# Linear attention ahead of two expert layers on one Trainium2 core: chunks 8 to 23 laid out by head group, with 8 loads a chunk instead of 15

## The chip, the core and the metric

The kernel runs on one core of a Trainium2 chip. The metric is device time in microseconds. One execution was taken by the hardware profiler; its trace is the source of every row below. The engines are TensorE (PE: matrix multiplies; PEld is its weight load), VectorE (DVE), ScalarE (ACT), GpSimd (POOL) and SyncE (SP), which here only issues DMAs.

## What is computed

Three stages follow one another over 3072 tokens. The first is attention with a decaying state, 4 batches of 8 heads of 768 steps, 64 wide; its output is the input of the second.

```python
# attention: gamma differs by head, scale = 1/8
for t in range(768):
    state = gamma * state + k[t] (x) v[t]        # 64 x 64 a head
    y[t] = scale * q[t] @ state
# second stage, x is y of all heads side by side: 3072 x 512
xn = x / sqrt(mean(x * x) + 1e-6) * rms_g
x = (silu(xn @ w_gate) * (xn @ w_val)) @ w_out   # 512 -> 1536 -> 512
# third stage
h = x @ w_in                                     # 512 -> 1024
s = h * softmax(h)
x = layernorm(s) * g_ln @ w_out2                 # 1024 -> 512
```

## The kernel before

The tokens are taken in 6 blocks of 512 (`NB`), the attention in 24 chunks of 128 (4 a block, `NCB`; 6 a batch, `CPB`). While TensorE works on block n, the attention of block n + 1 is done in small pieces that hang in numbered slots of block n (`extra`, run by `slot`). A scheduler then orders each engine's instructions; a piece that is written later comes later where two would compete.

The attention of chunks 0 to 3 and 4 to 7 has functions of its own (`first_...`, `unit_...`). Chunks 8 to 23 go through `att_load` (DMAs), `att_prep` (two products on GpSimd: the keys with their decay, `kd`, and the queries, `qd`), `att_scores` and `att_out`. Their matmuls are 64x64 and use the array as four quarters: the row half is the half of the 128 partitions that the operands stand in, the column half is the half that the result goes to, and `quads4` sets in which order the four take turns. `banks2` are the two result banks, SB and YB. A chunk's tiles are `rq`, `rk` (queries and keys for the scores), `rv` (keys and values for the state, in two blocks b of 64 rows), `qd`; each has 2 buffers, and chunk c + 2 is loaded after `att_out` of chunk c. In a name, `r` or `u` is a half of the rows or a head group of four heads, `pl` a pair of heads in it, `x` a head of a pair.

The state of chunks 0 to 7 has another layout than that of 8 to 23: at chunk 7 `decay_add` writes it over into `Uc`, and `turn_tables` loads the decay tables again in the second layout.

Between block n's attention and its second stage stands the normalisation over the tokens (`rms_1`, `rms_2`, `rms_mul`: the sums of squares `ssq` are gathered on TensorE, `rinv` is made on DVE and GpSimd and spread on TensorE in L374, and DVE multiplies `xT` by it in L378). The result is split into a rounded high half `xnh` (ACT) and a rest `xnl` (DVE), because each product is made of three matmuls (lines L806, L807, L808: high by high, low by high, high by low in some order). GB and VB hold the gate and value products, X the output product.

All weights come split in the same way. From the second block on they are reloaded from scratch in DRAM (`scr0`, `scr1` into `w4` tiles, 4 buffers; `scr2` into `wo` tiles, 2 buffers) in `w_load`, line L735. L620 stores sums of weights (`sscr`), L1121 loads tokens' sums (`t2scr`). In block 1 the weights of the third stage (`w2i`) are also brought in by L682 and converted. All of these and the chunk loads are issued by SyncE, one behind the other, and it waits at an instruction until its buffer is free; on top of that, eight completion semaphores take turns, so a DMA also waits for an earlier one that used its semaphore.

Of the kernel before, what the change touches and what calls it, by code (L numbers as in the profile page):

```python
# [42 lines left out]
def retention_moe_kernel(ctx: ExitStack, tc: tile.TileContext, qk0, q2, kt, kv, wpk, w2i, w2o,  # L43
                         rg, gl, sel, mtab, qtab, ktab, utab, out):
    nc = tc.nc
# [72 lines left out]
    def mm(out, lhsT, rhs, start, stop):  # L118
        return lambda: nc.tensor.matmul(out, lhsT=lhsT, rhs=rhs, start=start, stop=stop)  # L119

    def halfrows(hh):
        return slice(64 * hh, 64 * hh + 64)

    def decay_add(gc, r, ps, sv):

        old = U[gc % 2][r, ps, r]
        if gc == 2 * NCB - 1:
            u, x = ps.start // 2, r.start // 64
            for pl in range(2):
                new = Uc[0][halfrows(u ^ pl), 2 * pl + x, :]  # L130
                k = ps.start + pl
                nc.gpsimd.tensor_tensor(out=new, in0=U[gc % 2][r, k, r], in1=utab_t[r, k:k + 1].to_broadcast([64, 64]),
                                        op=ALU.mult)
                nc.vector.tensor_tensor(out=new, in0=new, in1=sv[:, pl, :], op=ALU.add)
            return
        new = U[(gc + 1) % 2][r, ps, r]
        if gc % CPB == 0:
            nc.vector.tensor_copy(new, sv)
        else:
            nc.gpsimd.tensor_tensor(out=new, in0=old,  # L140
                                    in1=utab_t[r, ps].unsqueeze(2).to_broadcast([64, ps.stop - ps.start, 64]),
                                    op=ALU.mult)
            nc.vector.tensor_tensor(out=new, in0=new, in1=sv, op=ALU.add)
# [77 lines left out]
    def att_load(gc):  # L221
        tq, tk = wt("rq", [P, 4, P], F32, 2), wt("rk", [P, 4, P], F32, 2)
        tv, qd = wt("rv", [P, 2, 2, 256], F32, 2), wt("qd", [P, 4, P], F32, 2)
        nc.sync.dma_start(tk, kt[gc])
        for u in range(2):
            nc.sync.dma_start(tq[halfrows(u)], q2[gc, u, 0:64])
        for r in range(2):
            for pl in range(2):
                xs_ = slice(128 * pl, 128 * pl + 128)
                for b in range(2):  # L230
                    src = kv[gc, r ^ pl, halfrows(b)].rearrange("j (t x) -> j t x", t=2)
                    nc.sync.dma_start(tv[halfrows(r), b, :, xs_], src[:, :, xs_])
        for r in range(2):
            for pl in range(2):
                src = q2[gc, r ^ pl, halfrows(r), 256 * pl:256 * pl + 256]
                nc.sync.dma_start(qd[halfrows(r), 2 * pl:2 * pl + 2, :], src.rearrange("d (h i) -> d h i", h=2))
        raw[gc] = (tq, tk, tv, qd)

    def turn_tables():

        for r in range(2):
            for pl in range(2):
                u, h = r ^ pl, 4 * (r ^ pl) + 2 * pl
                nc.sync.dma_start(m64[halfrows(r), u], mtab[halfrows(0), h:h + 2, 0:64])
                nc.sync.dma_start(ktab_t[halfrows(r), 2 * pl:2 * pl + 2], ktab[halfrows(1), h:h + 2])
                for x in range(2):
                    nc.sync.dma_start(qtab_t[halfrows(r), 2 * pl + x, 0:64], qtab[halfrows(x), h // 2, 0:64])
        nc.vector.tensor_scalar(u64, qtab_t[:, :, 63], 8.0, None, ALU.mult)

    def att_prep(gc):  # L250
# [10 lines left out]
        prepd[gc] = (tq, tk, tv, kd, qd)  # L261

    banks2 = (SB, YB)
    quads4 = ((1, 1), (0, 1), (1, 0), (0, 0))

    def half64(b):
        return slice(64 * b, 64 * b + 64)

    def state_mm(tv, kd, b):

        def one(r, pl, x):
            s = 2 * pl + x
            at = 256 + 128 * b + 64 * pl
            return mm(banks2[r][halfrows(r ^ x), at:at + 64], kd[halfrows(r), b, s, :],
                      tv[halfrows(r), b, 1, half64(s)], True, True)

        return [one(r, pl, x) for pl in range(2) for r, x in quads4]

    def state_add(new, b, copy=False):

        for r in range(2):
            for x in range(2):
                sv = banks2[r][halfrows(r ^ x), 256 + 128 * b:384 + 128 * b].rearrange("p (a e) -> p a e", a=2)
                out = new[halfrows(r), x::2, :]
                if copy:
                    nc.vector.tensor_copy(out, sv)
                else:
                    nc.vector.tensor_tensor(out=out, in0=out, in1=sv, op=ALU.add)
# [4 lines left out]
    def att_scores(gc):  # L293
        tq, tk, tv, kd, qd = prepd[gc]
        first = gc % CPB == 0

        def score(u, pl, x, b):
            at, hl = 128 * x + 64 * b, 2 * pl + x
            return mm(banks2[u][halfrows(u ^ pl), at:at + 64], tk[halfrows(u), hl, half64(b)],
                      tq[halfrows(u), hl, half64(b)], True, True)  # L300

        if not first:
            decay(Uc[1], Uc[0])
        run([score(u, pl, x, b) for b in range(2) for x in range(2) for u, pl in quads4] + state_mm(tv, kd, 0))
        gap("ga", 352)
        A = masked[gc] = wt("A", [P, 2, 2, P], F32, 2)
        for u in range(2):
            nc.vector.tensor_tensor(
                out=A[:, u].rearrange("p x (b i) -> p x b i", b=2),
                in0=banks2[u][:, 0:256].rearrange("p (x b i) -> p x b i", x=2, b=2),  # L310
                in1=m64[:, u].unsqueeze(2).to_broadcast([P, 2, 2, 64]), op=ALU.mult)
        state_add(Uc[1], 0, first)

    def out_calls(first, Y, Us, qd, v, A):
# [14 lines left out]
    def att_out(gc):  # L329
        tq, tk, tv, kd, qd = prepd.pop(gc)  # L330
        A = masked.pop(gc)
        first, last = gc % CPB == 0, gc % CPB == CPB - 1
        steps = [(0, b, pl) for b in range(1 if first else 0, 2) for pl in range(2)] \
            + [(1, b, pl) for b in range(2) for pl in range(2)]

        def one(i, r, x):
            kind, b, pl = steps[i]
            u, s = r ^ pl, 2 * pl + x
            at = 128 * u + 64 * b
            lhsT = tv[halfrows(r), b, 1, half64(s)] if kind else Uc[b][halfrows(r), s, :]  # L340
            rhs = A[halfrows(r), u, x, half64(b)] if kind else qd[halfrows(r), s, half64(b)]
            return mm(banks2[r][halfrows(x), at:at + 64], lhsT, rhs, i == 0, i == len(steps) - 1)

        calls = [one(i, r, x) for i in range(len(steps)) for r, x in quads4]
        if not last:
            calls += state_mm(tv, kd, 1)
        run(calls)
        if not last:
            decay(Uc[0], Uc[1])
            state_add(Uc[0], 1)  # L350
        cs = slice((gc % NCB) * P, (gc % NCB) * P + P)
        for r, ks in ((0, slice(0, 4, 3)), (1, slice(1, 3))):
            nc.scalar.copy(xT[:, ks, cs], banks2[r][:, 0:256].rearrange("p (u i) -> p u i", u=2))
        sq = wt("sq", [P, 512], F32, 1)
        for r in range(2):
            nc.scalar.activation(sq[:, 256 * r:256 * r + 256], banks2[r][:, 0:256], AF.Square)
        nc.gpsimd.tensor_tensor(out=xT[:, :, cs], in0=xT[:, :, cs], in1=rg_t.unsqueeze(2).to_broadcast([P, 4, P]),
                                op=ALU.mult)
        nc.vector.tensor_reduce(out=ssq[:, cs], in_=sq.rearrange("p (a i) -> p i a", a=4), axis=AX.X, op=ALU.add)
# [182 lines left out]
    def att_pieces(n):  # L542

        out = []
        if n == 1:
            units = [(gc, u) for gc in range(NCB, 2 * NCB) for u in range(2)]
            ahead = units + [(2 * NCB,), (2 * NCB + 1,)]
            for i, (gc, u) in enumerate(units):
                nxt, nx2 = ahead[i + 1], ahead[i + 2]

                def a(gc=gc, u=u, nxt=nxt):
                    unit_scores(gc, u)
                    if len(nxt) == 1:
                        turn_tables()

                def b(nxt=nxt):
                    (unit_prep if len(nxt) == 2 else att_prep)(*nxt)

                def c(gc=gc, u=u, nx2=nx2):
                    unit_out(gc, u)  # L560
                    (unit_load if len(nx2) == 2 else att_load)(*nx2)

                out += [a, b, c]
            return out
# [272 lines left out]
    extra = {}  # L837
# [679 lines left out]
```

## Time and profile before

| | |
|---|---|
| median of 3 runs | 988.19 us (987.37 to 989.81) |
| the profiled execution | 983.88 us |
| span of its trace | 982.1 us |
| mean granted TensorE clock | 0.991 of full |
| busy: PE, DVE, ACT, POOL | 958.7, 518.8, 408.7, 448.8 us |
| data moved | 231.95 MB, mean 236 GB/s |

The span is the time between the first and the last instruction of the trace; the execution's own time is a little longer. Busy shares are averages over stages. All times of a row are counted from the span's start.

### The profile page before, as it was taken

How to read it: one execution, taken by the hardware profiler on the slowest of the kernel's cores; microseconds unless marked ns; L12 is line 12 of the kernel's file. 1: busy time of each engine (PE TensorE's matmuls, PEld its weight loads, DVE VectorE, ACT ScalarE, POOL GpSimd, SP SyncE). 2: the span in 40 equal slices, each digit the busy share in tenths (PEclk: the TensorE clock that was granted, in tenths of full speed). 3: DMA queues.
4: the chain of work that ended last, by engine and by line, in shares of the span. 5: the costliest groups of instructions: out<-in, count | busy, mean ns of one | idle time of the engine just before them, and what ended most of it. 6: DMA issues, size and time to landing. Idle time of an engine off the chain costs nothing.

```text
span 982.1 us, 17723 instructions
## 1 busy us (share of the span) xinstructions
PE 958.7 (98%) x6636; PEld 797.5 (81%) x6636; DVE 518.8 (53%) x1040; ACT 408.7 (42%) x792; POOL 448.8 (46%) x494
## 2 busy tenths in 40 slices
PE   8999998999999999999899999999999999999998
PEld 7878786888888888888687888778788888899987
DVE  4798765562365744334574422576522456344473
ACT  4767655583334433222355221246312256321354
POOL 6886845582044495443437424527333426300022
PEclk9799999999999999999999999999999999999999
DMA  9699999996513215988933899761689954698501
GB/s 345 241 330 404 342 307 331 340 364 225 198 59 96 91 43 185 328 270 285 332 116 109 261 358 333 274 219 53 214 328 323 329 190 140 226 327 295 193 1 44
DMA packets 101334, 231.95 MB, mean 236 GB/s; under 512 B 13184, under 2 KB 43264, under 8 KB 100224
## 3 DMA queue, kind: packets, MB, share of 16 engines
q1 hardware_dynamic: 92464, 205.64, 61.1%
q10 hardware_dynamic: 8784, 25.17, 6.7%
q8 instruction: 53, 0.87, 0.4%
q14 instruction: 33, 0.27, 0.1%
HBM read 188.82 MB, written 41.94 MB: 235 GB/s over the span
## 4 chain that ended last, share of the span: by engine, by line
PE 74%; POOL 7%; DMA 6%; DVE 5%; ACT 3%; issue 3%; SPq 2%; ACTq 0%; POOLq 0%; DVEq 0%
PE X L806 9%; PE X L807 9%; PE X L808 9%; PE GB L806 6%; PE GB L808 6%; PE GB L807 6%; PE VB L806 5%; PE VB L807 5%; PE VB L808 5%; DMA wo<-scr 3%; PE X L1180 3%; PE VB L1180 2%; PE YB L119 2%; PE GB L1180 2%; PE VB L918 2%
## 5 line engine op out<-in xcount | busy, mean ns | idle before, releaser
L825 DVE TENSOR_TENSOR f<-VB,f 128x512 f32<-128x512 f32 x60 | 41.4, 690 | 133.4 <-PE VB L808 118.5
L806 PE MATMUL X<-r,wo 128*128 128x512 f32 x260 | 99.2, 396 | 5.3 <-DMA wo<-scr 5.3
L807 PE MATMUL X<-r,wo 128*128 128x512 f32 x260 | 102.7, 395 | 0.0
L808 PE MATMUL X<-r,wo 128*128 128x512 f32 x260 | 101.9, 392 | 0.0
L707 POOL TENSOR_TENSOR st<-st,x 128x512 int32<-128x512 int32 x52 | 69.9, 1346 | 54.0 <-ACT x L704 16.5
L854 ACT ACTIVATE f<-GB 128x512 f32<-128x512 f32 x60 | 35.7, 595 | 140.1 <-PE GB L808 140.1
L100 ACT CAST r<-f 128x512 fp32r<-128x512 f32 x72 | 44.6, 620 | 117.4 <-DVE f L825 99.2
L806 PE MATMUL GB<-xnh,w 128*128 128x512 f32 (+1 forms) x220 | 86.4, 393 | 2.3 <-ACT f L854 1.1
L807 PE MATMUL GB<-xnl,w 128*128 128x512 f32 (+1 forms) x220 | 86.2, 392 | 2.1 <-DVE xnl L101 2.0
L808 PE MATMUL GB<-xnh,w 128*128 128x512 f32 (+1 forms) x220 | 85.7, 390 | 0.1
L806 PE MATMUL VB<-xnh,w 128*128 128x512 f32 (+1 forms) x220 | 85.6, 389 | 0.0
L808 PE MATMUL VB<-xnh,w 128*128 128x512 f32 (+1 forms) x220 | 85.1, 387 | 0.3 <-POOL w L101 0.3
L807 PE MATMUL VB<-xnl,w 128*128 128x512 f32 (+1 forms) x220 | 85.0, 386 | 0.0
L101 DVE TENSOR_TENSOR r<-f,r 128x512 fp32r<-128x512 f32 x72 | 61.1, 849 | 30.2 <-ACT r L100 29.5
L602 POOL TENSOR_TENSOR x<-x 128x512 f32<-128x512 f32 x24 | 31.1, 1298 | 88.6 <-DMA x<-scr 49.0
L806 PEld LDWEIGHTS X<-r,wo 128*128 128x128 f32 x260 | 49.1, 189 | 16.0 <-issue 5.6
L291 POOL TENSOR_TENSOR U<-U,u 128x256 f32<-128x256 f32 x27 | 16.9, 627 | 98.6 <-PE SB L119 65.1
L101 POOL TENSOR_TENSOR r<-st,r 128x512 fp32r<-128x512 f32 x8 | 10.3, 1290 | 109.6 <-ACT r L100 109.6
L806 PE MATMUL X<-w2oh,r 128*128 128x512 f32 (+1 forms) x144 | 57.0, 396 | 1.4 <-ACT r L1051 0.8
L808 PEld LDWEIGHTS X<-r,wo 128*128 128x128 f32 x260 | 49.1, 189 | 10.2
L807 PEld LDWEIGHTS X<-r,wo 128*128 128x128 f32 x260 | 49.3, 189 | 10.1 <-issue 0.2
L808 PE MATMUL X<-w2oh,r 128*128 128x512 f32 (+1 forms) x144 | 55.7, 387 | 0.0
(458 smaller groups left out, 2533.7 us busy)
## 6 DMA issues: line engine op xcount, KB each, us to landing
w<-scr SPq DMA_DIRECT2D x96, 512.0 KB, 6.5
wo<-scr SPq DMA_DIRECT2D x59, 512.0 KB, 5.8
x<-in_wpk SPq DMA_DIRECT2D x36, 512.0 KB, 6.1
x<-scr SPq DMA_DIRECT2D x25, 512.0 KB, 5.9
sscr<-x SPq DMA_DIRECT2D x24, 512.0 KB, 8.3
scr<-CV ACTq DMA_DIRECT2D x18, 512.0 KB, 6.0
rv<-in_kv SPq DMA_DIRECT2D x128, 64.0 KB, 2.3
scr<-w ACTq DMA_DIRECT2D x12, 512.0 KB, 5.7
```

The source lines that it names most:

```text
L100: h = nc.scalar.copy(hi, src)
L101: (lo_eng or nc.vector).tensor_tensor(out=lo, in0=src, in1=hi.bitcast(F32), op=ALU.subtract)
L119: return lambda: nc.tensor.matmul(out, lhsT=lhsT, rhs=rhs, start=start, stop=stop)
L602: nc.gpsimd.tensor_tensor(out=w[:, 0, :], in0=w[:, 0, :], in1=w[:, 1, :], op=ALU.add)
L707: nc.gpsimd.tensor_tensor(out=ti, in0=ti, in1=lo, op=ALU.add)
L806: nc.tensor.matmul(ps, lhsT=lh, rhs=rh, start=start, stop=False)
L807: nc.tensor.matmul(ps, lhsT=lh, rhs=rl, start=False, stop=False)
L808: return nc.tensor.matmul(ps, lhsT=ll, rhs=rh, start=False, stop=stop)
L825: recent["dve"] = nc.vector.tensor_tensor(out=a, in0=GV[1], in1=silu[:, 0, :], op=ALU.mult)
L854: recent["act"] = nc.scalar.activation(s[:, 0, :], GV[0], AF.Silu)
L918: nc.tensor.matmul(ps, lhsT=x, rhs=y[:, k, :], start=start and k + i == 0, stop=k == 1 and i == 2, skip_group_check=True)
L1180: last["mm"] = nc.tensor.matmul(bank, lhsT=x[:, k, ts_], rhs=y[:, k, :], start=start and k + i == 0, stop=k == 1 and i == 2, skip_group_ch ...
```

## The change

For chunks 8 to 23, values, keys for the state, states and `qd` now stand in row halves by head group (group 0 above, group 1 below); before, each half held one pair of each group. The queries and keys of the scores stand in row halves by pair. The result bank is in each case that of the row half. With that a chunk's tiles are filled by 8 DMAs over 64 rows each (two each for `rk`, `rq`, `rv`, `qd`) instead of 15 (1, 2, 8, 4); the bytes are the same. The runs of one row that a DMA copies are 2 KB for `rv` instead of 512 B, 2 KB for `qd` instead of 1 KB, and 1 KB for `rk` and `rq` instead of 2 KB. `turn_tables` has 8 DMAs instead of 16, `decay_add` at chunk 7 four GpSimd and four DVE instructions instead of eight of each, and ScalarE's copies into `xT` write neighbouring columns. In `att_out` the block b = 1 of the state comes ahead of b = 0. `att_prep` of chunk 8, which hung in a slot of block 0 ahead of the normalisation, hangs in a slot of block 1. Numbers of matmuls are unchanged.

```diff
 def decay_add(gc, r, ps, sv):
     if gc == 2 * NCB - 1:
-        u, x = ps.start // 2, r.start // 64
-        for pl in range(2):
-            new = Uc[0][halfrows(u ^ pl), 2 * pl + x, :]
-            k = ps.start + pl
-            nc.gpsimd.tensor_tensor(out=new, in0=U[gc % 2][r, k, r], in1=utab_t[r, k:k + 1].to_broadcast([64, 64]),
-                                    op=ALU.mult)
-            nc.vector.tensor_tensor(out=new, in0=new, in1=sv[:, pl, :], op=ALU.add)
-        return
+        new = Uc[0][halfrows(ps.start // 2), r.start // 64::2, :]
 def att_load(gc):
-        nc.sync.dma_start(tk, kt[gc])
+        ktu = kt[gc].rearrange("(u d) y -> d u y", u=2)
+        for pl in range(2):
+            nc.sync.dma_start(tk[halfrows(pl)].rearrange("p (u x) i -> p u (x i)", u=2), ktu[:, :, 256 * pl:256 * pl + 256])
+            nc.sync.dma_start(tq[halfrows(pl)].rearrange("p (u x) i -> p u (x i)", u=2),
+                              q2[gc, :, 0:64, 256 * pl:256 * pl + 256].rearrange("u d y -> d u y"))
         for u in range(2):
-            nc.sync.dma_start(tq[halfrows(u)], q2[gc, u, 0:64])
-        for r in range(2):
-            for pl in range(2):
-                xs_ = slice(128 * pl, 128 * pl + 128)
-                for b in range(2):
-                    src = kv[gc, r ^ pl, halfrows(b)].rearrange("j (t x) -> j t x", t=2)
-                    nc.sync.dma_start(tv[halfrows(r), b, :, xs_], src[:, :, xs_])
-        for r in range(2):
-            for pl in range(2):
-                src = q2[gc, r ^ pl, halfrows(r), 256 * pl:256 * pl + 256]
-                nc.sync.dma_start(qd[halfrows(r), 2 * pl:2 * pl + 2, :], src.rearrange("d (h i) -> d h i", h=2))
+            nc.sync.dma_start(tv[halfrows(u)].rearrange("p b t y -> p b (t y)"),
+                              kv[gc, u].rearrange("(b j) y -> j b y", b=2))
+            nc.sync.dma_start(qd[halfrows(u)], q2[gc, u, 0:64].rearrange("d (h i) -> d h i", h=4))
-    quads4 = ((1, 1), (0, 1), (1, 0), (0, 0))
+    quads4 = ((0, 1), (1, 1), (0, 0), (1, 0))
 def att_scores(gc):
-        def score(u, pl, x, b):
-            at, hl = 128 * x + 64 * b, 2 * pl + x
-            return mm(banks2[u][halfrows(u ^ pl), at:at + 64], tk[halfrows(u), hl, half64(b)],
-                      tq[halfrows(u), hl, half64(b)], True, True)
+        def score(pl, u, x, b):
+            at, hl = 128 * x + 64 * b, 2 * u + x
+            return mm(banks2[pl][halfrows(u), at:at + 64], tk[halfrows(pl), hl, half64(b)],
+                      tq[halfrows(pl), hl, half64(b)], True, True)
 def att_out(gc):
-        steps = [(0, b, pl) for b in range(1 if first else 0, 2) for pl in range(2)] \
+        steps = [(0, b, pl) for b in ((1,) if first else (1, 0)) for pl in range(2)] \
             + [(1, b, pl) for b in range(2) for pl in range(2)]
-        def one(i, r, x):
+        def one(i, u, x):
             kind, b, pl = steps[i]
-            u, s = r ^ pl, 2 * pl + x
-            at = 128 * u + 64 * b
-            lhsT = tv[halfrows(r), b, 1, half64(s)] if kind else Uc[b][halfrows(r), s, :]
-            rhs = A[halfrows(r), u, x, half64(b)] if kind else qd[halfrows(r), s, half64(b)]
-            return mm(banks2[r][halfrows(x), at:at + 64], lhsT, rhs, i == 0, i == len(steps) - 1)
+            s, at = 2 * pl + x, 128 * pl + 64 * b
+            lhsT = tv[halfrows(u), b, 1, half64(s)] if kind else Uc[b][halfrows(u), s, :]
+            rhs = A[halfrows(u), pl, x, half64(b)] if kind else qd[halfrows(u), s, half64(b)]
+            return mm(banks2[u][halfrows(x), at:at + 64], lhsT, rhs, i == 0, i == len(steps) - 1)
 def att_pieces(n):
                 def b(nxt=nxt):
-                    (unit_prep if len(nxt) == 2 else att_prep)(*nxt)
+                    if len(nxt) == 2:
+                        unit_prep(*nxt)
+                    else:
+                        extra.setdefault((1, 2), []).insert(0, lambda: att_prep(*nxt))
```

The instructions' order on an engine shows where this moves them. The changed kernel's line numbers are lower by 7 to 13 (L236 becomes L225, L232 becomes L223, L735 becomes L725).

First place: SyncE near the end of block 2, where a chunk's `qd` and `rv` loads stand ahead of the block's last two `wo` tiles (from `scr_2_119` and `scr_2_122`). Before:

```order
L236 DMA qd_4590<-in_q 64x256 x4
L232 DMA rv_4589<-in_kv 64x2x128 x8
L735 DMA wo_4651<-scr_2_119 128x1024
L1121 DMA w_539_4667<-t2scr_135 128x1024
L620 DMA sscr_1_124<-x_535_4645 128x1024
L620 DMA sscr_1_124<-x_536_4648 128x1024
L1121 DMA w_540_4668<-t2scr_135 128x1024
L735 DMA wo_4711<-scr_2_122 128x1024
```

and with the change:

```order
L225 DMA qd_4511<-in_q 64x512 x2
L223 DMA rv_4510<-in_kv 64x2x512 x2
L725 DMA wo_4565<-scr_2_119 128x1024
L1111 DMA w_539_4581<-t2scr_135 128x1024
L610 DMA sscr_1_124<-x_535_4559 128x1024
L610 DMA sscr_1_124<-x_536_4562 128x1024
L1111 DMA w_540_4582<-t2scr_135 128x1024
L725 DMA wo_4625<-scr_2_122 128x1024
```

Nothing changes its place; twelve chunk loads become four. The same stands one block on.

Second place: TensorE at the passage from block 0 to block 1, where L374 (then L361) spreads `rinv` and the first GB matmul of block 1 reads a `w` tile. Before:

```order
L808 MATMUL X_71<-r_201_1609,wo_1438 128x512
L806 MATMUL VB<-xnh,CV 128x512
...
L806 MATMUL VB<-xnh,CV 128x512
L374 MATMUL SB<-ident,rinv 128x128 x4
L807 MATMUL VB<-xnl,CV 128x512
L808 MATMUL VB<-xnh,CV 128x512
L806 MATMUL GB<-xnh,w_203_1629 128x512
L807 MATMUL GB<-xnl,w_203_1629 128x512
```

and with the change:

```order
L798 MATMUL GB<-xnh,CV 128x512
L361 MATMUL SB<-ident,rinv 128x128 x4
L796 MATMUL VB<-xnh,CV 128x512
...
L798 MATMUL VB<-xnh,CV 128x512
L796 MATMUL GB<-xnh,w_202_1596 128x512
L119 MATMUL SB<-rq_1415,rk_1416 64x64
L797 MATMUL GB<-xnl,w_202_1596 128x512
```

All twelve VB matmuls now stand behind the four of `rinv`; before, ten of them stood ahead. On DVE at the same place, before:

```order
L706 TENSOR_SCALAR st_1489<-x_182_1386 128x512
L719 SCALAR_TENSOR_TENSOR st_1443<-st_1443,YB 128x512
L368 TENSOR_SCALAR rinv<-SB 128x4
L101 TENSOR_TENSOR CV<-st_1443,CV 128x512
L248 TENSOR_SCALAR u_146<-qtab_t 128x4
L719 SCALAR_TENSOR_TENSOR st_1489<-st_1489,YB 128x512
L378 SCALAR_TENSOR_TENSOR xT<-xT,rg_t,SB 128x512 x4
L825 TENSOR_TENSOR f_204_1643<-VB,f_204_1643 128x512
L101 TENSOR_TENSOR xnl<-xT,xnh 128x512 x4
```

and with the change:

```order
L355 TENSOR_SCALAR rinv<-SB 128x4
L696 TENSOR_SCALAR st_1470<-x_182_1386 128x512
L709 SCALAR_TENSOR_TENSOR st_1432<-st_1432,YB 128x512
L101 TENSOR_TENSOR CV<-st_1432,CV 128x512
L709 SCALAR_TENSOR_TENSOR st_1470<-st_1470,YB 128x512
L365 SCALAR_TENSOR_TENSOR xT<-xT,rg_t,SB 128x512 x4
L101 TENSOR_TENSOR xnl<-xT,xnh 128x512
```

`rinv` went ahead of two steps of a weight conversion, and `xnl` ahead of the product `f`.

Third place: SyncE at the start of block 1; the first `w` tiles come from `scr_0_87` and `scr_1_88`, those of TensorE's next GB and VB groups from `scr_0_90` and `scr_1_91`. Before:

```order
L735 DMA w_203_1629<-scr_0_87 128x1024
L735 DMA w_205_1649<-scr_1_88 128x1024
L682 DMA x_206_1651<-in_w2i 128x512
L735 DMA w_210_1690<-scr_0_90 128x1024
L682 DMA x_211_1692<-in_w2i 128x512
L735 DMA wo_1738<-scr_2_89 128x1024
L735 DMA w_218_1740<-scr_1_91 128x1024
L682 DMA x_222_1769<-in_w2i 128x512
```

and with the change:

```order
L725 DMA w_202_1596<-scr_0_87 128x1024
L725 DMA w_204_1616<-scr_1_88 128x1024
L672 DMA x_205_1618<-in_w2i 128x512
L225 DMA qd_1548<-in_q 64x512 x2
L223 DMA rv_1547<-in_kv 64x2x512 x2
L672 DMA x_210_1659<-in_w2i 128x512
L725 DMA wo_1705<-scr_2_89 128x1024
L672 DMA x_221_1736<-in_w2i 128x512
L672 DMA x_228_1769<-in_w2i 128x512
L725 DMA w_209_1657<-scr_0_90 128x1024
```

The reload from `scr_0_90` moved behind three more `w2i` loads; the loads of chunk 9, which stood ahead of all of these, stand among them.

## Rows read from the trace of the kernel before

**Rows 1.** The page, part 1: busy us, share of the span, instructions.
```profile
PE 958.7 (98%) x6636; PEld 797.5 (81%) x6636; DVE 518.8 (53%) x1040; ACT 408.7 (42%) x792; POOL 448.8 (46%) x494
```
**Rows 2.** TensorE's waits: us in total, times, longest.
```profile
PE X L806 <- DMA wo<-scr: 5.3, 2, 3.1
...
PE GB L807 <- DVE xnl L101: 2.0, 1, 2.0
...
PE X L1180 <- POOL r L101: 1.0, 1, 1.0
```
**Rows 3.** The chain that ended last, 465 to 486: start, us, what.
```profile
466.82 0.23 PE X L808
...
470.09 8.92 DMA wo<-scr
...
479.15 0.77 PE X L806
...
482.45 0.24 PE X L807
```
**Rows 4.** Timeline of SyncE, 453 to 484: start, us, what, count.
```profile
455.22 2.64 SPq L236 DMA_DIRECT2D qd<-in_q  x4
458.25 7.96 SPq L232 DMA_DIRECT2D rv<-in_kv  x8
466.31 0.54 SPq L735 DMA_DIRECT2D wo<-scr  x1
...
470.09 1.63 SPq L735 DMA_DIRECT2D wo<-scr  x1
```
**Rows 5.** DMA, 455 to 480 in 40 slices of 0.625 us.
```profile
GB/s 249 311 321 413 400 433 387 375 315 251 121 143 95 42 2 105 105 105 131 109 179 374 321 151 170 197 269 380 393 367 393 426 413 426 420 406 360 439 419 452
```
**Rows 6.** The chain that ended last, 620 to 660.
```profile
625.40 0.24 PE X L808
...
626.27 10.51 DMA wo<-scr
...
636.91 0.47 PE X L806
```
**Rows 7.** Timeline of SyncE, 612 to 656.
```profile
616.11 7.41 SPq L232 DMA_DIRECT2D rv<-in_kv  x8
623.62 0.53 SPq L735 DMA_DIRECT2D wo<-scr  x1
```
**Rows 8.** Timeline of TensorE, 156.5 to 165.5, in brackets idle before and releaser.
```profile
158.75 0.49 PE L806 MATMUL GB<-xnh,w 128*128 128x512 f32 x1 [1.02 <-ACT xnh L100]
161.27 0.67 PE L807 MATMUL GB<-xnl,w 128*128 128x512 f32 x1 [2.03 <-DVE xnl L101]
...
165.02 0.40 PE L806 MATMUL GB<-xnh,w 128*128 128x512 f32 x1
```
**Rows 9.** Timeline of DVE, 140 to 176.
```profile
151.78 0.15 DVE L368 TENSOR_SCALAR rinv<-SB 128x4 f32<-128x4 f32 x1
...
157.29 2.72 DVE L378 SCALAR_TENSOR_TENSOR xT<-xT,rg_t,SB 128x512 f32<-128x512 f32 x4 [3.37 <-PE SB L374]
```
**Rows 10.** Timeline of GpSimd, 140 to 176.
```profile
146.92 1.29 POOL L707 TENSOR_TENSOR st<-st,x 128x512 int32<-128x512 int32 x1 [3.94 <-DMA scr<-w]
...
152.66 1.48 POOL L369 TENSOR_TENSOR rinv<-rinv,mhalf 128x4 f32<-128x4 f32 x1
```
**Rows 11.** Instructions of line L232: ns min, median, max.
```profile
L232 SPq DMA_DIRECT2D rv<-in_kv x128: 533/600/1410, 130.1 to 700.0; - x128
```
**Rows 12.** Timeline of SyncE, 135 to 190.
```profile
163.87 0.33 SPq L682 DMA_DIRECT2D x<-in_w2i  x1
```
**Rows 13.** Timeline of GpSimd, 625 to 668.
```profile
651.68 1.29 POOL L259 TENSOR_TENSOR qd<-qd,qtab_t 128x512 f32<-128x512 f32 x1 [4.68 <-DMA qd<-in_q]
```
**Rows 14.** Timeline of TensorE, 475.2 to 475.45, two of the small matmuls.
```profile
475.24 0.22 PE L119 MATMUL YB<-rq,rk 64*64 64x64 f32 x1
...
475.30 0.22 PE L119 MATMUL YB<-rq,rk 64*64 64x64 f32 x1
```

More of the change, by code (lines that the diff above doesn't have):

```diff
@@ L126, in decay_add @@
         old = U[gc % 2][r, ps, r]
+        new = U[(gc + 1) % 2][r, ps, r]
         if gc == 2 * NCB - 1:
-            u, x = ps.start // 2, r.start // 64
-            for pl in range(2):
-                new = Uc[0][halfrows(u ^ pl), 2 * pl + x, :]
-                k = ps.start + pl
-                nc.gpsimd.tensor_tensor(out=new, in0=U[gc % 2][r, k, r], in1=utab_t[r, k:k + 1].to_broadcast([64, 64]),
-                                        op=ALU.mult)
-                nc.vector.tensor_tensor(out=new, in0=new, in1=sv[:, pl, :], op=ALU.add)
-            return
-        new = U[(gc + 1) % 2][r, ps, r]
+            new = Uc[0][halfrows(ps.start // 2), r.start // 64::2, :]
         if gc % CPB == 0:
@@ L237, in att_load @@
+        for u in range(2):
+            nc.sync.dma_start(tv[halfrows(u)].rearrange("p b t y -> p b (t y)"),
+                              kv[gc, u].rearrange("(b j) y -> j b y", b=2))
+            nc.sync.dma_start(qd[halfrows(u)], q2[gc, u, 0:64].rearrange("d (h i) -> d h i", h=4))
         raw[gc] = (tq, tk, tv, qd)
     def turn_tables():
[L241 to L247, printed above, removed]
+        for u in range(2):
+            nc.sync.dma_start(m64[halfrows(u)].rearrange("p a x i -> p (a x) i"),
+                              mtab[halfrows(0), 4 * u:4 * u + 4, 0:64])
+            nc.sync.dma_start(ktab_t[halfrows(u), 0:4], ktab[halfrows(1), 4 * u:4 * u + 4])
+            for x in range(2):
+                nc.sync.dma_start(qtab_t[halfrows(u), x::2, 0:64], qtab[halfrows(x), 2 * u:2 * u + 2, 0:64])
@@ L269, in state_mm, with one @@
     def state_mm(tv, kd, b):
-        def one(r, pl, x):
+        def one(u, pl, x):
             s = 2 * pl + x
             at = 256 + 128 * b + 64 * pl
-            return mm(banks2[r][halfrows(r ^ x), at:at + 64], kd[halfrows(r), b, s, :],
-                      tv[halfrows(r), b, 1, half64(s)], True, True)
-        return [one(r, pl, x) for pl in range(2) for r, x in quads4]
+            return mm(banks2[u][halfrows(u ^ x), at:at + 64], kd[halfrows(u), b, s, :],
+                      tv[halfrows(u), b, 1, half64(s)], True, True)
+        return [one(u, pl, x) for pl in range(2) for u, x in quads4]
     def state_add(new, b, copy=False):
[L281 to L284, printed above, removed]
+        for u in (1, 0):
+            for x in (0, 1):
+                sv = banks2[u][halfrows(u ^ x), 256 + 128 * b:384 + 128 * b].rearrange("p (a e) -> p a e", a=2)
+                out = new[halfrows(u), x::2, :]
                 if copy:
@@ L295, in att_scores @@
         first = gc % CPB == 0
-        def score(u, pl, x, b):
-            at, hl = 128 * x + 64 * b, 2 * pl + x
-            return mm(banks2[u][halfrows(u ^ pl), at:at + 64], tk[halfrows(u), hl, half64(b)],
-                      tq[halfrows(u), hl, half64(b)], True, True)
+        def score(pl, u, x, b):
+            at, hl = 128 * x + 64 * b, 2 * u + x
+            return mm(banks2[pl][halfrows(u), at:at + 64], tk[halfrows(pl), hl, half64(b)],
+                      tq[halfrows(pl), hl, half64(b)], True, True)
         if not first:
             decay(Uc[1], Uc[0])
-        run([score(u, pl, x, b) for b in range(2) for x in range(2) for u, pl in quads4] + state_mm(tv, kd, 0))
+        run([score(pl, u, x, b) for b in range(2) for x in range(2) for pl, u in quads4] + state_mm(tv, kd, 0))
         gap("ga", 352)
         A = masked[gc] = wt("A", [P, 2, 2, P], F32, 2)
-        for u in range(2):
+        for pl in (1, 0):
             nc.vector.tensor_tensor(
-                out=A[:, u].rearrange("p x (b i) -> p x b i", b=2),
-                in0=banks2[u][:, 0:256].rearrange("p (x b i) -> p x b i", x=2, b=2),
-                in1=m64[:, u].unsqueeze(2).to_broadcast([P, 2, 2, 64]), op=ALU.mult)
+                out=A[:, pl].rearrange("p x (b i) -> p x b i", b=2),
+                in0=banks2[pl][:, 0:256].rearrange("p (x b i) -> p x b i", x=2, b=2),
+                in1=m64[:, pl].unsqueeze(2).to_broadcast([P, 2, 2, 64]), op=ALU.mult)
         state_add(Uc[1], 0, first)
@@ L332, in att_out @@
         first, last = gc % CPB == 0, gc % CPB == CPB - 1
-        steps = [(0, b, pl) for b in range(1 if first else 0, 2) for pl in range(2)] \
+        steps = [(0, b, pl) for b in ((1,) if first else (1, 0)) for pl in range(2)] \
             + [(1, b, pl) for b in range(2) for pl in range(2)]
-        def one(i, r, x):
+        def one(i, u, x):
             kind, b, pl = steps[i]
-            u, s = r ^ pl, 2 * pl + x
-            at = 128 * u + 64 * b
-            lhsT = tv[halfrows(r), b, 1, half64(s)] if kind else Uc[b][halfrows(r), s, :]
-            rhs = A[halfrows(r), u, x, half64(b)] if kind else qd[halfrows(r), s, half64(b)]
-            return mm(banks2[r][halfrows(x), at:at + 64], lhsT, rhs, i == 0, i == len(steps) - 1)
-        calls = [one(i, r, x) for i in range(len(steps)) for r, x in quads4]
+            s, at = 2 * pl + x, 128 * pl + 64 * b
+            lhsT = tv[halfrows(u), b, 1, half64(s)] if kind else Uc[b][halfrows(u), s, :]
+            rhs = A[halfrows(u), pl, x, half64(b)] if kind else qd[halfrows(u), s, half64(b)]
+            return mm(banks2[u][halfrows(x), at:at + 64], lhsT, rhs, i == 0, i == len(steps) - 1)
+        calls = [one(i, u, x) for i in range(len(steps)) for u, x in quads4]
         if not last:
@@ L351, in att_out @@
         cs = slice((gc % NCB) * P, (gc % NCB) * P + P)
-        for r, ks in ((0, slice(0, 4, 3)), (1, slice(1, 3))):
-            nc.scalar.copy(xT[:, ks, cs], banks2[r][:, 0:256].rearrange("p (u i) -> p u i", u=2))
+        for u in range(2):
+            nc.scalar.copy(xT[:, 2 * u:2 * u + 2, cs], banks2[u][:, 0:256].rearrange("p (a i) -> p a i", a=2))
         sq = wt("sq", [P, 512], F32, 1)
```

## Prediction

> **What bounds the kernel now.** I read the page first: TensorE is busy for 98% of the span [rows 1]. No other engine is near that, so only two things can shorten the run: less time in which TensorE stands still, and less time in which it runs at its lower clock. The work of TensorE itself isn't changed here. So the second view is the table of TensorE's waits [rows 2]. Most of its entries are a start-up or a one-off of 1 us; three can be touched by this change. The loads of an output weight tile `wo` hold it up twice, 5.3 us in all and 3.1 at the longest; the low half `xnl` of the normalised tokens once, for 2.0; a GpSimd subtraction once, for 1.0. Three places follow, read in the chain that ended last and in the timelines.
>
> *Place A, at 476 us.* TensorE ends a run of X matmuls at 467.05 and then has other work; the next X group starts at 479.15, because a `wo` load issued at 470.09 took 8.92 us to land [rows 3]. The wait is the longest of the two, 3.1 us, so TensorE was ready for it at about 476.05. Then TensorE is at the lower of its two clocks (1.2 against 2.4 GHz): seven matmuls start between 479.15 and 482.45, 3.30 us where seven at 0.23 take 1.6. So the wait costs 3.1 + 1.7 = 4.8 us. Why is the load late? SyncE's own queue [rows 4] shows that eight `rv` loads of 64 KB keep it from 458.25 for 7.96 us, four `qd` loads before them for 2.64, and that six transfers of 0.5 MB follow in one heap, the first at 466.31, the last (the late one) at 470.09. While the small loads are issued the queues run nearly empty: the eleven slices from 461.25 to 468.13 have 2 to 179 GB/s, about 105 the most common, where the heap later moves 380 to 450 [rows 5]. So SyncE's issuing bounds that stretch, and the heap behind it is landed late.
>
> *Place B, at 635 us.* The same picture one block on: X ended at 625.64, `wo` was issued at 626.27, took 10.51 us, and the X group started at 636.91 [rows 6]. The wait is 5.3 - 3.1 = 2.2 us; the next matmuls run at 0.23, so no clock is lost. Eight `rv` loads stand ahead from 616.11 for 7.41 us [rows 7].
>
> *Place C, at 158 us.* The start of block 1 waits for its normalisation: 1.02 us for `xnh`, then 2.03 for `xnl`, and afterwards nine matmuls start between 161.27 and 165.02, 3.75 us instead of 2.1, at the lower clock [rows 8]. That is 3.05 + 1.7 = 4.7 us. The chain behind it: DVE reads the sums of squares at 151.78, GpSimd takes the power at 152.66 to 154.14, TensorE spreads it in L374, DVE scales `xT` from 157.29 [rows 9, 10].
>
> **The change part by part.** *The loads.* A chunk loses 15 DMAs and gets 8 of the same bytes. One DMA over 64 rows holds SyncE for 600 ns at the median [rows 11]. Eight `rv` at that price are 4.8 us and the two that replace them 1.2, so 3.6 us go; four `qd` become two, 1.2 us less. `rk` in two pieces instead of one costs more, bounded by nothing and by one more such DMA, 0.6; I take 0.3. Net about -4.5 us of SyncE a chunk, and up to 6.8 us where the queue is as slow as at 458 (7.96 - 1.2). Most of that is hidden, since TensorE waits at A and B alone; there it counts.
>
> At A the order of issues is unchanged (the first pair of order rows above). The last `wo` can't go before X ends at 467.05, so it gains 470.09 - 467.05 = 3.0 us; and of the six transfers the first two needn't wait for it, so about 1 MB is out of its way, 2.5 us at 400 GB/s. It would land at 479.0 - 5.5 = 473.5, and TensorE wants it at 476.05. Margin 2.5 us: I take 4.3 of the 4.8, bounds 0 (if the DMA engines alone set the landing) and 4.8.
> At B the issue gains only 0.6 us (X ended at 625.64), the rest must come from the shorter heap: the earlier `wo`, issued at 623.62, could go at about 617.3 (616.11 + 1.2), as could the tile behind it. 0.6 + 2.5 = 3.1 against a wait of 2.2; a thin margin. I take 2.0, bounds 0.6 and 2.2.
>
> The Trainium skill speaks against this (DMA: Bandwidth & Descriptors, section Issuing engines are not separate DMA queues): the sequencer time to start a DMA is usually small against the DMA itself. By that rule A and B would keep their waits, and the sum of 11.0 below would be 4.7 (C and the small wait at 654). Behind it stand the rows: 7.96 us of issuing for 0.5 MB, beside 1.3 us for 0.5 MB at 400 GB/s, so here the trace disagrees; the same rule as a mechanism of this kernel is rival 2 below.
>
> *Chunk 8's preparation.* Its `kd` and `qd` products (two GpSimd instructions, 1.3 us each by [rows 13]) are now written behind the normalisation, and the scheduler puts them into GpSimd's idle 3.94 us ahead of 146.92 [rows 10]. On DVE `rinv` goes ahead of two steps that it stood behind (L706 and L719, the second pair of order rows); from 151.78 I put it at about 150.1. On GpSimd the power then follows at about 150.2, with two instructions fewer between it and 146.92. On TensorE L374 (after: L361) stands ten matmuls earlier in the stream (the same pair), 2.3 us: at about 154.0, with its 0.94 us and twelve VB matmuls (2.7 us) behind it instead of two. So DVE's `xT` starts at 155.0, not 157.29; it took 1.46 us from there to the first GB matmul (158.75), and TensorE now gets there at 157.7, behind its cover. The first `xnl` follows `xT` directly on DVE, ahead of the product `f` of 0.68 us. I keep a wait of 0.5: gain 4.2, bounds 0 (if chunk 8's loads are late, the two products now stand ahead of `rinv`) and 4.7. Without the twelve VB matmuls as cover the gain would shrink by 2.7.
>
> *The 1.0 us at 654.* X waits for a GpSimd subtraction, which stands behind `qd`'s product, which waited 4.68 us for its load [rows 2, 13]. Two `qd` loads instead of four land earlier; by how much no row says. Half: 0.5, bounds 0 and 1.0.
>
> *The rest: nothing.* The 64x64 matmuls, masks, state updates and copies have the same shapes and numbers, apart from four POOL and DVE pairs fewer at chunk 7 and half the table loads, in block 0, where no wait of TensorE hangs on them. The four quarters of the array still take turns: the next four matmuls start 0.06 us after four others [rows 14], and in the old order as in the new one neighbours differ in row half each time, and share a column half every second time.
>
> Sum: 4.3 + 2.0 + 4.2 + 0.5 = 11.0 us. Each wait removed brings TensorE sooner to loads that took 9 to 10 us in these stretches; for what waits next I allow 0.7 at each of three places, a choice and not a reading: -2.2. So 8.8 us, from the profiled 983.88 to 975.1. The median of the runs is 4.31 above the profiled run, so 988.19 - 8.8 = 979.4.
>
> **The rivals.**
> 1. *Half of it.* The issues go earlier, but at B or at C the wait stays (thin margin at B; at C GpSimd's products wait for chunk 8's loads). For it: B's margin is 0.9 us, and C needs four engines in step. Gain 3.5 to 6: 982 to 985.
> 2. *Nothing measurable.* The bytes are the same and the heap is 3 MB; if the DMA engines and not SyncE set its landing, A and B keep their waits, and C's gain is lost in block 1's loads. For it: landings of 9 to 10 us [rows 3, 6]; against it the 105 GB/s [rows 5]. Within 2 us of before: about 987.
> 3. *Weights late in block 1.* The third pair of order rows: the reload that feeds TensorE's second GB group (`scr_0_90`) now stands behind four `w2i` loads that wait for conversion buffers, where one stood ahead of it. If the fourth is issued as late as before (163.87, [rows 12]) and lands like `wo` at A (8.92), it is there at 172.8. TensorE would want it at 157.7 + 37 x 0.23 + 0.5 = 166.7: 6.1 us of waiting and 1.7 at the lower clock, 7.8. It decides from an issue later than 157.8. Against it: SyncE is free about 8 us sooner there. It eats all but 1 us of the gain: 979.4 + 7.8 = 987.2.
> 4. *Slower: the quarters fall out of step.* If the swapped halves made neighbours in the stream wait for each other, each of 1,024 small matmuls (64 a chunk, 16 chunks) would start 0.03 us after the last instead of 0.015: 15 us on TensorE itself, spread over all blocks, 979.4 + 15 = 994. It decides from 0.009 us more for each. Only the symmetry above speaks against it.
>
> **How the numbers follow.** Forecast 0.52, with a range of its own of 976 to 982; rival 1 0.21; rival 2 0.12; rival 3 0.08; rival 4 or another new wait that outweighs the gain 0.07. About 0.3% (3 us) is what timing can tell from no change, so faster means under 985.2. Rival 2 with the greater part of rival 3 is no change. Faster 0.74, no change 0.17, slower 0.09. The low end is all bounds met: 4.8 + 2.2 + 4.7 + 1.0 = 12.7 gives 975.5; the high end takes in rivals 2 and 3 up to 988.
>
> **What would show it.** Right: `rv` takes SyncE about 1.2 us at 458; the waits for `wo` fall from 5.3 to under 1; L361 runs at about 154; the lower clock is gone after 158 and 476. Wrong: `wo` still landing after TensorE's need (rival 2), a wait of GB for `w` near 167 (rival 3), 64x64 matmuls spaced wider than 0.06 us in four (rival 4).

## The result and the profile after

The changed kernel takes 980.46 us (median of 4, 979.02 to 981.35) against 988.36 for the kernel before (median of 4): a ratio of 0.9918 with an interval of 0.99 to 0.9935, 7.9 us faster. The forecast was 979.4, and 8.8 us. Two more sets of runs gave ratios of 0.9923 (0.9893 to 0.9952) and 0.9948 (0.992 to 0.9975).

The profiled execution took 980.58 us, near that median. The one of before, 983.88, did not: it lies under all of the first timed runs of its kernel (987.37 to 989.81). So the two traces are 3.4 us of span apart where the medians are 7.9. The page of the changed kernel, its first lines [rows 1]:

```profile
span 978.7 us, 17532 instructions
...
PE 961.2 (98%) x6636; PEld 799.3 (82%) x6636; DVE 523.4 (53%) x1036; ACT 407.2 (42%) x792; POOL 452.5 (46%) x490
```

TensorE's waits of the changed kernel (total, times, longest), which answer to [rows 2]:

```profile
PE X L1170 <- POOL r L101: 3.4, 2, 1.9
PE YB L119 <- DVE st L709: 1.5, 1, 1.5
...
PE X L796 <- ACT r L100: 0.9, 1, 0.9
```

The 5.3 us for `wo` and the 2.0 for `xnl` are gone. The wait for GpSimd's `r` has grown from 1.0 to 3.4, and one of 1.5 is new. SyncE's timeline at place A, to be read beside [rows 4]:

```profile
454.70 1.77 SPq L225 DMA_DIRECT2D qd<-in_q  x2
456.57 1.29 SPq L223 DMA_DIRECT2D rv<-in_kv  x2
458.32 0.33 SPq L725 DMA_DIRECT2D wo<-scr  x1
461.04 0.33 SPq L1111 DMA_DIRECT2D w<-t2scr  x1
463.54 1.34 SPq L610 DMA_DIRECT2D sscr<-x  x2
465.30 0.32 SPq L1111 DMA_DIRECT2D w<-t2scr  x1
466.75 0.32 SPq L725 DMA_DIRECT2D wo<-scr  x1
```

The loads of `rv` hold SyncE for 1.29 us instead of 7.96. The six large transfers are no longer one heap between 466.31 and 470.09; they go out one by one from 458.32 to 466.75, each when its own condition is met. At place B [rows 7] the same:

```profile
613.61 1.29 SPq L223 DMA_DIRECT2D rv<-in_kv  x2
616.00 0.32 SPq L725 DMA_DIRECT2D wo<-scr  x1
...
624.43 0.32 SPq L725 DMA_DIRECT2D wo<-scr  x1
```

TensorE at place C, 154 to 163, which answers to [rows 8]:

```profile
156.79 1.05 PE L361 MATMUL SB<-ident,rinv 128*128 128x128 f32 x8
157.60 0.48 PE L796 MATMUL VB<-xnh,CV 128*128 128x512 f32 x1
...
160.44 0.49 PE L796 MATMUL GB<-xnh,w 128*128 128x512 f32 x1
160.86 0.33 PE L119 MATMUL SB<-rq,rk 64*64 64x64 f32 x2
161.25 0.50 PE L797 MATMUL GB<-xnl,w 128*128 128x512 f32 x1
```

Twelve VB matmuls from 157.60 on cover the work of DVE and ACT, and neither GB matmul has a bracket with a wait. What came in exchange stands at 494. GpSimd's timeline, and behind it TensorE's:

```profile
491.85 0.72 POOL L247 TENSOR_TENSOR qd<-qd,qtab_t 128x256 f32<-128x256 f32 x1 [6.22 <-DMA qd<-in_q]
492.53 1.27 POOL L101 TENSOR_TENSOR r<-st,r 128x512 fp32r<-128x512 f32 x1
```
```profile
493.85 0.73 PE L1170 MATMUL X<-w2ih,r 128*128 128x512 f32 x2 [1.87 <-POOL r L101]
```

GpSimd sat 6.22 us until a `qd` load had landed, then made `qd`, and only then the rest `r` that TensorE wants. Before, the wait for `wo` stood ahead of this place and hid it. The chain of work at this place shows why the load was late:

```profile
472.81 11.78 DMA w<-scr
...
484.60 7.18 DMA qd<-in_q
```

The second of the two `qd` loads was issued only at 484.60, when a `w` reload issued at 472.81 had landed; in the program that reload stands eight DMAs ahead of it, so the load takes over its completion semaphore. At 651 it is the same: a reload issued at 630.49 took 11.81 us, and the `qd` load behind it went out at 642.32. The clock tells the rest; columns of the windows are length, busy time (and instructions) of PE, PEld, DVE, ACT, POOL, then the granted clock, the DMA share and GB/s:

```profile
50.00:75.00 25.00, 23.39 (x114) 18.48 (x113) 21.79 (x29) 15.55 (x27) 19.71 (x15) 0.93 0.93 330
...
150.00:175.00 25.00, 24.02 (x107) 18.78 (x107) 16.60 (x23) 15.66 (x27) 12.30 (x9) 1.00 0.98 340
...
475.00:500.00 25.00, 23.03 (x210) 18.18 (x205) 16.31 (x41) 9.46 (x20) 6.75 (x8) 0.93 0.62 182
```

In this trace the lower clock is gone after place C, but it is back behind the wait at 494, and once at 68, behind a wait of 1.15 us for GpSimd. 0.93 over 25 us is a loss of about 1.7 us each time.

From the first attention matmul of block 0 with a wait (65.76 before, 66.03 after; the block 0 mark from here on) to the end are 916.3 us before and 912.7 after, 3.7 less. The larger items add up to that: A gives 3.08 + 1.7, B 2.27, C 3.05 + 1.7 less 0.90 for ACT's `r`; the wait at 494 takes 1.87 + 1.7, the one at 651 grows by 0.5 (1.02 to 1.50), the new one at 226 takes 1.5 and the clock at 68 1.7. Sum 3.7. Smaller waits are left out; they are together about 1 us less in the changed kernel, so the sum is good to about 1 us.

### The profile page after: what moved, and what is told of

It reads as the page before. It is cut to its first block, busy times and chain, and to the rows that moved or that the text cites. A ratio compares the mean times of both kernels' runs of the same rounds, so it can differ in the third digit from the quotient of the medians.

```text
span 978.7 us, 17532 instructions
## 1 busy us (share of the span) xinstructions
PE 961.2 (98%) x6636; PEld 799.3 (82%) x6636; DVE 523.4 (53%) x1036; ACT 407.2 (42%) x792; POOL 452.5 (46%) x490
## 4 chain that ended last, share of the span: by engine, by line
PE 76%; DMA 7%; POOL 7%; DVE 4%; ACT 3%; issue 2%; SPq 1%; ACTq 0%; POOLq 0%; DVEq 0%
PE X L796 9%; PE X L798 9%; PE X L797 9%; PE GB L796 6%; PE GB L797 6%; PE GB L798 6%; PE VB L796 5%; PE VB L797 5%; PE VB L798 5%; PE X L1170 3%; DMA w<-scr 2%; PE SB L119 2%; PE VB L1170 2%; PE VB L908 2%; PE YB L908 2%
## 5 line engine op out<-in xcount | busy, mean ns | idle before, releaser
L797 PE MATMUL X<-w2ol,r 128*128 128x512 f32 (+1 forms) x144 | 55.3, 384 | 0.0
```

The costliest lines, as they stand in the source:

```text
L797: nc.tensor.matmul(ps, lhsT=lh, rhs=rl, start=False, stop=False)
```

## The experiments

All ratios are to the kernel before on the same chip, with 95% intervals.

**control.** No edit: the kernel before. 

> The kernel before, once more, for a second trace of it. Theory (the traced execution of before, 983.88, was an early finisher: its timed runs read 987.4 to 989.8): the ratio is 1.000 within 0.2%, the new trace has a span of 985 to 988, and the 2 to 5 us that it is longer than 982.1 are one or two more stretches at the lower clock or longer waits at start-up, in places that have nothing to do with the loads. Rival: the span is 982 again and the timed runs are longer outside it.

Measured 987.63 us, ratio 0.9996 (0.9977 to 1.0016), span 985.9. From the block 0 mark (67.17) to the end it has 918.7 us. Its waits:

```profile
PE X L806 <- DMA wo<-scr: 5.2, 2, 2.9
...
PE GB L806 <- DMA w<-scr: 1.9, 1, 1.9
```

So A and B are not chance, and C is there too, with a wait for the first `w` tile in place of `xnh`. The theory holds for where the longer execution lost time: the start (1.4 us up to the mark, and a stretch of low clock at 70). Three traces of the changed kernel have 912.7, 910.5 and 910.4 from the mark to the end, against 916.3 and 918.7: 3.7 to 8.3 us apart, about 6.3 on the mean of each. That is near what the three sets of medians give (7.9, 6.7 and 6.5).

**small_rows.** Sixteen loads, `rv` and `qd` cut by rows, all runs as long as in the changed kernel.

```diff
-            nc.sync.dma_start(tv[halfrows(u)]..., kv[gc, u].rearrange("(b j) y -> j b y", b=2))
-            nc.sync.dma_start(qd[halfrows(u)], q2[gc, u, 0:64]...)
+            for c in range(4):   # 16 rows each
+                nc.sync.dma_start(tv[64 * u + 16 * c : ... + 16]..., kv[gc, u]...[16 * c : 16 * c + 16])
+        for u in range(2):
+            for c in range(2):   # 32 rows each
+                nc.sync.dma_start(qd[64 * u + 32 * c : ... + 32], q2[gc, u, 32 * c : 32 * c + 32]...)
```

> The changed kernel with its rv in eight loads of 16 rows and its qd in four of 32 rows: 16 loads a chunk, the copied runs as long as in the changed kernel (2 KB). Theory (the number of issues on SyncE made wo late): the waits for wo at about 476 and 635 come back, 2 to 3 us each, the time is 983 to 987, 3 to 6 above the changed kernel. Rival (short 512 B runs kept the DMA engines slow): no wait for wo, the time within 1.5 us of the changed kernel.

Measured 991.17 us, ratio 1.0036 (1.0014 to 1.0058): all of the gain is gone and more, twice what was expected. TensorE's waits, then SyncE's timeline at place A:

```profile
PE X L801 <- DMA wo<-scr: 7.9, 3, 4.4
```
```profile
457.64 2.07 SPq L230 DMA_DIRECT2D qd<-in_q  x4
460.62 8.14 SPq L225 DMA_DIRECT2D rv<-in_kv  x8
468.86 0.37 SPq L730 DMA_DIRECT2D wo<-scr  x1
...
472.69 1.63 SPq L730 DMA_DIRECT2D wo<-scr  x1
```

The picture of before is back, with bytes and runs as in the changed kernel, and in the new layout, so the layout by itself gives nothing. TensorE's and DVE's orders differ from the changed kernel's mostly in blocks 0 and 1, and not at A. The number of loads makes it; the rival of short runs falls for A and B. But the instructions of one line at that place (count, ns min, median, max) show that my wording of the mechanism was off. In the kernel before, and in small_rows:

```profile
L232 SPq DMA_DIRECT2D rv<-in_kv x8: 533/576/602, 458.2 to 465.6; - x8
```
```profile
L225 SPq DMA_DIRECT2D rv<-in_kv x8: 311/373/431, 460.6 to 468.3; - x8
```

A load of 16 rows takes SyncE a third less, 3.0 us for eight instead of 4.6, and yet the eight take 8.14 us instead of 7.96. The rest is SyncE waiting, in the waits of SyncE at that place, before and in small_rows:

```profile
SPq L232 <- DMA w<-scr: 2.8, 3, 1.6
...
SPq L232 <- DMA wo<-scr: 0.7, 1, 0.7
```
```profile
SPq L225 <- DMA w<-scr: 4.7, 3, 2.7
SPq L225 <- DMA wo<-scr: 1.1, 1, 1.1
```

A load has to wait for an earlier, large DMA to land, whose completion semaphore it takes over: in the program each DMA waits for the one eight places ahead of it. Of before's 7.96 us about 4.6 are issuing, and such waits (3.5 in the view) make up the rest. In the changed kernel the four loads at A wait for no DMA.

**small_runs.** The same number, but `rv` in eight loads with runs of 512 B and `qd` in four with 1 KB, as before, in the new layout.

```diff
+            for c in range(2):
+                for b in range(2):
+                    nc.sync.dma_start(tv[halfrows(u), b, :, 128 * c:128 * c + 128],
+                                      kv[gc, u, halfrows(b)]...[:, :, 128 * c:128 * c + 128])
```

> The changed kernel with its rv in eight loads of 512 B runs and its qd in four of 1 KB runs, as before, in the new layout: 16 loads a chunk. Theory (number of issues): as small_rows, 983 to 987 with both waits for wo; the normalisation at block 1 is spread late again in TensorE's order, so about 3 to 5 us of waiting there too, up to 989. Rival (short runs): waits for wo here and not in small_rows.

Measured 999.03 us, ratio 1.0111 (1.0083 to 1.0139), 10 us above what was expected and 8 above small_rows. TensorE's waits:

```profile
PE X L802 <- DMA wo<-scr: 11.2, 5, 4.9
...
PE VB L802 <- DMA w<-scr: 2.3, 2, 1.9
```

More reloads are late than in small_rows. The scheduler orders this kernel otherwise in many places, and `rinv`'s matmuls stand late in TensorE's stream again, so this run doesn't say how much of the 8 us is due to short runs and how much to the order. That stays open.

**rest_dve**, and **after_pair** beside **rest_pair.** One rest of the third stage is made on DVE; the other engines' orders stay the same, row for row.

```diff
-        S4 = parts(s4, nc.gpsimd)
+        S4 = parts(s4, nc.vector)
```

> The changed kernel with one of the split rests of the third stage (S4) made on DVE instead of GpSimd, where it stands behind a product that waits for a qd load; all other orders are the same. Theory (what the loads gave at 476 and 635 was taken back at 494 and 651 by that GpSimd queue): the waits of X for GpSimd's r, 1.9 and 1.5 us in the changed kernel's trace, go, and with them a stretch at the lower clock; 3 to 5 us less, 975.5 to 977.5. Rival (another wait of the same chain takes their place, DVE being late): within 1 us of 980.5.

Measured 976.43 us, ratio 0.9888 (0.9858 to 0.9917). DVE and GpSimd at the place of 494 (here at 491 to 497, this execution being 1.0 us later at the block 0 mark and 4.8 us later at place C):

```profile
491.40 0.69 DVE L101 TENSOR_TENSOR r<-st,r 128x512 fp32r<-128x512 f32 x1 [0.69 <-ACT r L100]
```
```profile
496.81 0.74 POOL L247 TENSOR_TENSOR qd<-qd,qtab_t 128x256 f32<-128x256 f32 x1 [6.42 <-DMA qd<-in_q]
```

GpSimd still waits 6.42 us for `qd`, but `r` is ready nearly five us ahead of it and TensorE has no wait there or at 651. On one chip beside the changed kernel:

> The changed kernel, on one chip with rest_pair, to compare the two directly. Theory (the GpSimd queue takes back part of the gain): 979 to 982, 3 to 5 us above rest_pair.

> The changed kernel with the S4 rest on DVE, beside after_pair on one chip. Theory: 3 to 5 us below it, and no wait of X for GpSimd's r. Rival (rest_dve's 976.4 was chance between chips): within 1.5 us of after_pair.

after_pair 981.91 us, ratio 0.9948 (0.992 to 0.9975); rest_pair 976.43, ratio 0.9872 (0.9852 to 0.9892). The intervals don't touch: 5.5 us, and this version beats both kernels. The two profiled executions do not show it: both have a span of 975.9. The one of after_pair waited only 1.6 us for `r`, without a clock loss behind it, and reached the block 0 mark 2.3 us sooner (65.48 against 67.82). So the gain in time is shown, and that the waits for `r` go with it; that they are the whole of it is not. In the three traces of the changed kernel these waits are 3.4, 2.9 and 1.6 us, and only the first has the 1.7 us of clock behind them; from the block 0 mark on, the mean of the three is 911.2 us and that of rest_dve and rest_pair 909.4. Four of the nine executions of after_pair took 986 to 988 us, the other five 978 to 982, and the traced one is the shortest of all: where the long ones lose their time no trace shows.

**rest_old.** The same edit in the kernel before. 

> The kernel before, with the S4 rest on DVE as in rest_dve. Theory (that GpSimd queue limits only once the wo waits ahead of it are gone): it saves the 1.0 us of the one wait there, 987 to 988.5. Rival (it is worth 4 us by itself and has nothing to do with the loads): 983 to 985.

Measured 988.93 us, ratio 1.001 (0.9992 to 1.0028): nothing at all. Its waits for `wo`:

```profile
PE X L806 <- DMA wo<-scr: 7.2, 3, 3.5
```

The 1.0 us for `r` is gone, and the waits for `wo` are 1.9 longer. The edit is worth 4.0 (rest_dve beside the first runs of the changed kernel, on another chip) to 5.5 us behind the new loads and nothing ahead of them.

**mid_rows.** Ten loads: `rv` in four of 32 rows. Here TensorE's and DVE's orders are those of the changed kernel.

```diff
-            nc.sync.dma_start(tv[halfrows(u)]..., kv[gc, u]...)
+            for c in range(2):   # 32 rows each
+                nc.sync.dma_start(tv[64 * u + 32 * c : ... + 32]..., kv[gc, u]...[32 * c : 32 * c + 32])
```

> The changed kernel with rv in four loads of 32 rows instead of two of 64: 10 loads a chunk, two more; TensorE's and DVE's orders are row for row the same. Theory (SyncE's issuing, with a margin at 476 that two more issues of 0.6 to 1 us don't use up): no wait for wo at 476 and under 0.5 us at 634, within 1.5 us of after_again. Rival (every load counts, as the 10.7 us for eight more in small_rows would say): a quarter of that, 2.7 us more, with waits for wo.

Measured 983.85 us, ratio 0.9958 (0.9937 to 0.9979), beside 0.9923 (0.9893 to 0.9952) for the changed kernel on that chip: 3 us more at the median, with intervals that overlap. That is the time of the rival (2.7) and not of the theory (within 1.5), but the overlap leaves it open. The trace has no wait for `wo` at A and 0.31 us at B, as the theory said. What it has besides is GpSimd's queue again, and TensorE's wait for it:

```profile
649.35 1.26 POOL L249 TENSOR_TENSOR qd<-qd,qtab_t 128x512 f32<-128x512 f32 x1 [6.51 <-DMA qd<-in_q]
```
```profile
PE X L1172 <- POOL r L101: 2.7, 1, 2.7
```

**after_again.** No edit: the changed kernel. 

> The changed kernel once more, for a second trace and on the same chip as the next two. Theory (the waits for wo are gone for good, and what differs between executions is start-up and the start of block 1): 979 to 982; no wait of X for wo, 1.5 to 1.9 us twice of X for GpSimd's r near 494 and 651, and between 1 and 3 us of waits at 150 to 166. Rival (the 158 us place was cured as forecast): under 1 us there again.

Measured 980.82 us, ratio 0.9923. No wait for `wo`; 1.00 and 1.86 us for `r`; at block 1 0.74 us, where the theory said 1 to 3. In the traces of this kernel and of rest_dve, which has the same order there, the waits from 148 to 167 sum to 0.90, 0.74, 2.48, 3.05 and 1.77 us, against 3.30 and 3.64 in two of before. These are other waits than before, nearly all for ScalarE's `r` and for the sums of squares; those for `xnh` are gone and those for `xnl` at most 0.18 us. In the traces with 2.48 and 3.05 us (after_pair and rest_dve) the lower clock is back too; here that of after_pair:

```profile
150.00:175.00 25.00, 24.53 (x103) 19.56 (x104) 15.96 (x21) 15.62 (x27) 12.25 (x9) 0.93 0.94 317
```

So C is cured in part, in some executions nearly whole, in others hardly. ScalarE in the worst of them (rest_dve) shows what decides:

```profile
144.51 0.61 ACT L100 CAST wo<-st 128x512 fp32r<-128x512 f32 x1
149.97 0.33 ACTq L742 DMA_DIRECT2D scr<-w  x1
150.39 0.37 ACT L208 COPY xT<-SB 128x256 f32<-128x256 f32 x1 [5.26 <-DMA rk<-in_kt]
```

ScalarE stands still for 5.26 us: the store that it issues at 149.97 waits for an `rk` load of SyncE to land (eight DMAs ahead of it in the program), and the copy of `xT` behind it begins the whole normalisation. In all five traces this store goes out within 0.2 us of that load's landing, which took 7.7, 7.8, 8.1, 9.3 and 8.8 us (in the order of the sums above). The third trace has a larger wait than the second because TensorE lost no clock at 68 there and came to this place 1.8 us sooner behind the block 0 mark than in the first.

## Why the prediction was right, step by step

*The loads and place A: right in size, the cause half right.* The wait went whole (4.8 of 4.8 us; 4.3 was taken). The last `wo` was issued at 466.75, where 467.05 had been worked out: 3.3 us sooner than before, 3.0 taken. The shorter heap gave less than its 2.5 us: the tile took 8.1 us to land instead of 8.92, so it was there at 474.9 and not at 473.5, 0.8 us ahead of the first matmul that reads it (475.67). What failed is the sentence that SyncE's issuing bounds that stretch. Issuing is about 4.6 of the 7.96 us; the rest is waiting for large DMAs to land, and small_rows, with the issuing cut by a third and the same total, shows that cheaper issues alone did not help. Fewer loads took away both.

*Place B: right.* 2.27 us, 2.0 taken. The thin margin showed itself: two more loads bring 0.31 us back (mid_rows).

*Place C: near in size in the first trace, by luck, and wrong in cause.* 3.8 us there (4.7 less 0.90), 4.2 taken; in after_pair, with 2.48 us of waits and the clock lost, it is about 0.6. And I gave the credit to the moved preparation of chunk 8. With that move undone, the order of instructions on TensorE, DVE, GpSimd and SyncE comes out the same, row for row; with it made in the old kernel, also. The move does nothing. What brought `rinv`'s matmuls ahead of the twelve VB matmuls is the scheduler, to which the loads look different: they stand early with ten loads and with sixteen by rows, and late with sixteen in short runs. Why it does so is not shown. The times that I worked out for it were 2.8 us too early (L361 at 154.0; it ran at 156.79), and the wait went anyway, since TensorE was late as well: 0.27 us at the block 0 mark, 1.7 of clock at 68 and the new wait of 0.90.

*The 1.0 us at 654: wrong sign.* I expected half of it to go. It became 3.4 us at two places, and 1.7 of lost clock: `qd` landed no sooner relative to TensorE, because TensorE itself arrived sooner and because at both places the second of its two loads still had to wait for a reload to land. This is what the allowance of 2.2 us stood for, and it was too small: with the 1.5 us at 226, where the scores of chunk 8 now come early and wait for the bank YB that a weight conversion still reads, 5.5 us were given back.

*The sum: near in part by luck.* In the first trace A, B and C gave 10.9 us (10.5 were taken), but with what was given back and the clock at 68 the traced gain from the block 0 mark on is 3.7 us, not 8.8. The traced execution was forecast at 975.1 and took 980.58. The median fell by 7.9 all the same, because the traced execution of before was a short one, 4.3 us under its median: others lose more, as control does, mostly in places that the sum of 11.0 doesn't hold. From the mark on, the mean gain of all traces (two of before, three of the changed kernel) is about 6.3 us.

*The rivals.* Rival 1 came nearest, in C alone and by run. Rival 2 fell with A and B. The prediction set against the bytes alone what the Trainium skill says (DMA: Bandwidth & Descriptors, section Issuing engines are not separate DMA queues), that the time to start a DMA is usually small beside the DMA, and found that the trace disagrees. For a single load the trace agrees: at A before, 0.58 us of SyncE and 3.4 us to landing, both medians of the eight. What made A late is that eight stood behind one another, with waits among them. Rival 3 fell: the reload in question was issued from 156.53, ahead of the 157.8 from which it would have decided:

```profile
156.53 3.61 SPq L725 DMA_DIRECT2D w<-scr  x2
```

Rival 4 fell: the first of each four small matmuls follow at 0.06 us, as in [rows 14]:

```profile
474.91 0.22 PE L119 MATMUL SB<-rq,rk 64*64 64x64 f32 x1
...
474.97 0.22 PE L119 MATMUL SB<-rq,rk 64*64 64x64 f32 x1
```

## What to carry to other kernels

Where many small loads stand ahead of a large one in the same queue, count what each of them waits for, not only what it costs to issue: here 15 loads merged into 8 of the same bytes took two late tiles off the bounding engine. A wait that is removed uncovers the next one behind it, so look in the trace for queues that wait without cost today (GpSimd for `qd`, 3.9 us at 494 in the kernel before) and have them ready: that was worth 4.0 to 5.5 us more, and nothing without the first step. And don't credit a line of the diff with what a scheduler does: undo it and compare the orders of the instructions.

## What the runs showed of the hardware that was not expected

The profiled execution may be an unusual one: from the block 0 mark to the end, two executions of the kernel before differ by 2.4 us and three of the changed one by 2.3, and what differs between them is one or two stretches of lower clock (1.7 us each) and the landing times of single loads. A DMA that one engine issues can wait for one that another has issued: ScalarE's store of block 0 stood 5.26 us for a load of SyncE, because the program takes its eight completion semaphores in turn. And eight loads of 16 rows, each issued in 0.37 us, took as long (8.14 us) as eight of 64 rows at 0.58 (7.96), because of those same waits.
